# The gMLP row mix's quarter loads: a second place for a21, asked for a pair ahead; a11 asked for ahead of a22

## The chip, the cores and the metric

One core of one Trainium2 chip. The metric is device time in microseconds (us) of one execution of the whole program; lower is better.

## The reference

One sequence of 2048 rows of width 512, all in float32. An attention block, then a gated MLP whose gate mixes rows:

```python
h  = x + attention(layernorm(x)) @ wo            # 32 heads of 16
z  = gelu(layernorm(h) @ w_in)                   # 1376 columns: z1 (688), then z2 (688)
g  = w_sp @ layernorm(z2) + b_sp[:, None]        # w_sp is 2048 x 2048
h2 = h + (z1 * g) @ w_out
```

The change concerns the product `w_sp @ layernorm(z2)`.

## The kernel before

The program runs through four stages: the projections, attention, `make_z` (the MLP's input product, the gelu and the layernorm, up to 1595 us of the span), and the row mix with the output product (from there to the end). Float32 matmuls are made of three: each operand is split into a rounded part and a rest (`parts`: ScalarE writes the rounded part, VectorE the rest), and `mm3` (L87, L88, L89) multiplies high by high, high by low and low by high.

The row mix multiplies by halves with seven products in place of eight. `w_sp` is cut into quarters a11, a12, a21, a22 of 1024 x 1024, and layernorm(z2) into b11, b12, b21, b22 of 1024 x 344. For each **pair** p of row blocks (block p of the upper half and block p of the lower, 128 rows each, p = 0 to 7) the left operands are

- s3 = a11 - a21 (`difference`, L761),
- s1 = a21 + a22, written over a21, and s2 = s1 - a11, written over a11 (`sums`, L761); s2 is also stored to `s_scr` (L783),
- a22 itself, and later a11, a12 and s4 = a12 - s2.

The loop over p from L895 (`for p in range(HB)`) makes four of the products, in TensorE's order g7 = s3 x t3, g6 = s2 x t2, g4 = a22 x n4, g5 = s1 x t1, each of 24 matmuls (8 blocks, three each) of 344 columns. `T` holds t1, t2, t3 and n4, the right operands, made of b. While TensorE makes the products of pair p, the other engines prepare the operands of pair p + 1: `put` splits an operand into one of six places (the slots w0 to w2 and f0 to f2, in rotation). ScalarE's order in one turn of the loop is: the splits of s3, s2, one block of b11 and a22, then `p6` (L952, the copy of g6 out of PSUM), then the split of s1. VectorE's order is: s3, its rest, the sums, the rests of s2, b11 and a22, then `p67` (L953), the rest of s1, and last the three sums `q` (L903, in `keep`) that empty g4 and g5. These orders, and those of TensorE and of the queue SP that issues the loads, are the order of the code (`manual_schedule`): an instruction that waits holds back all behind it on its engine.

PSUM has four buffers for g. The first product of the next pair takes the buffer of g6, which `p6` frees; the second takes that of g7, freed by `p67`; the third and fourth those of g4 and g5, freed by `q`.

A quarter's rows come as two loads of 128 x 512 float32 (256 KB each). `ask(i, j, p, tag)` takes places from a pool by its tag and issues both loads (L747). Tag "rc" has two tiles, so one place, which holds a21; it is free again when both parts of s1 have been made. Tag "o" has one place for a22, free when a22 has been split. Tag "xr" has three tiles for a11, which needs two: the next a11's first half goes into the third tile, its second half into the tile of the present first half, free when s2 has been split and stored. In each turn p, SP issues in this order: the two stores of s2 (L783), the two loads of a22 of pair p + 2, the two of a11, the two of a21, one of b (L874), and the three stores of g (L904).

The last turn (p = 7) has other work: it puts a11 of pair 0 into slot f0 (asked for in turn 6 at the tag "rc"), then splits the sixteen blocks b22 and b21 into the memory of t3 (free after g7) and of t2 (free after g6). Their loads run through six tiles: the sixth b22 block's load waits until the last b11 block has been split, and each of the later ten until a block six earlier has been split. Behind eight of these ten comes a load of 1 MB of w_out (L948), then the last two. The stores of the last g and a reload of pair 0's (`qz`, L980) stand behind those. Then the final loop begins: g1 = a11 x b11, g3 = s4 x b22, g2 = a12 x b21 for each pair, the gate, and the output product; its first transposes (L1035) need `pr`, VectorE's product with z1 (L1073).

Of the kernel before, what the change touches and what calls it, by code (L numbers as in the profile page):

```python
# [8 lines left out]
F32 = mybir.dt.float32  # L9
# [9 lines left out]
P = 128  # L19
# [25 lines left out]
def block_kernel(ctx: ExitStack, tc: tile.TileContext, x, wqkv, wo, w_in, w_sp4, b_sp, w_out, out):  # L45
# [200 lines left out]
    with ExitStack() as pre:  # L246
# [163 lines left out]
        with tc.manual_schedule(engines={E.PE, E.Activation, E.DVE, E.SP}):  # L410
# [47 lines left out]
            for g in range(3):  # L458
                a, b = 4 * g, 4 * g + 4
# [44 lines left out]
            for j in range(24):  # L504
                b, n, i = 1 + j // 8, j // 2 % 4, 1 - j % 2
# [29 lines left out]
    e2 = late.enter_context(tc.tile_pool(name="early_2", bufs=2))  # L535
# [189 lines left out]
    QB = HB // 2  # L725
# [11 lines left out]
    def parts(hi, lo, src, el=None, eh=None):  # L737
        if eh == "pool":
            nc.gpsimd.tensor_copy(hi, src)
        else:  # L740
            nc.scalar.activation(hi, src, AF.Copy)  # L741
        (nc.gpsimd if el == "pool" else nc.vector).tensor_sub(lo, src, hi.bitcast(F32))  # L742

    def load_a(halves, i, j, p):

        for n, t in enumerate(halves):
            nc.sync.dma_start(t, w_sp4[p + HB * i][:, HB * j + QB * n:HB * j + QB * n + QB, :])  # L747

    def cut(t):
        return [t[:, QB * n:QB * n + QB, :] for n in range(2)]  # L750

    def put(slot, halves):

        op = slot.take()
        for n in range(2):
            parts(cut(op[0])[n], cut(op[1])[n], halves[n])
        return op

    def combine(e, out, a, b, op):
        for n in range(2):  # L760
            e.tensor_tensor(out[n], a[n], b[n], op)  # L761

    def half(name, tag, bufs=2):
        return [e2.tile([P, QB, P], F32, name=name, tag=tag, bufs=bufs) for _ in range(2)]

    def ask(i, j, p, tag):

        t = half(f"a{i}{j}", tag, 3 if tag == "xr" else 2)
        load_a(t, i, j, p)
        return t  # L770

    def difference(a11, a21):

        s3 = [e2.tile([P, QB, P], F32, name="s3", tag=f"o2{n}", bufs=1) for n in range(2)]
        combine(nc.vector, s3, a11, a21, ALU.subtract)
        return s3

    def sums(p, a11, a21, a22):

        combine(nc.vector, a21, a21, a22, ALU.add)  # L780
        combine(nc.vector, a11, a21, a11, ALU.subtract)
        for n in range(2):
            nc.sync.dma_start(cut(s_scr[p])[n], a11[n])  # L783

    with ExitStack() as mid:
# [57 lines left out]
        for k in range(NB):  # L843
# [8 lines left out]
            if k == NB - 2:  # L852
                a11, a21, a22 = ask(0, 0, 0, "xr"), ask(1, 0, 0, "rc"), ask(1, 1, 0, "o")
# [6 lines left out]
    with ExitStack() as fin:  # L860
        bc = fin.enter_context(tc.tile_pool(name="fin_b", bufs=1, side="right"))
        fs = fin.enter_context(tc.tile_pool(name="fin_s", bufs=1, side="right"))
        f1 = late.enter_context(tc.tile_pool(name="fin_1", bufs=2))
# [5 lines left out]
        def load_b(i, j, k):  # L869

            staged[0] += 1
            t = (f1.tile([P, FC], F32, name="b", bufs=3) if staged[0] % 2 else
                 e2.tile([P, FC], F32, name="b", tag="hn", bufs=3))
            nc.sync.dma_start(t, z_scr[1][(HB * i + k) * P:(HB * i + k + 1) * P, j * FC:(j + 1) * FC])  # L874
            return t
# [3 lines left out]
        def put_b(b, k, t):  # L879
            parts(b[0][:, k, :], b[1][:, k, :], t)  # L880

        def product(acc, a, b, blocks=range(HB)):
            for k in blocks:
                mm3(acc, a[0][:, k, :], a[1][:, k, :], b[0][:, k, :], b[1][:, k, :],
                    k == 0, k == HB - 1)
# [3 lines left out]
        f = [Slot(fs, f"f{i}") for i in range(3)]  # L889
        ops["s1"] = put(f[0], a21)  # L890
        old, now = [None, None, f[1], f[2]], w + f[:1]
        order = fin.enter_context(tc.manual_schedule(engines={E.PE, E.Activation, E.DVE, E.SP}))
        a11, a21, a22 = ask(0, 0, 1, "xr"), ask(1, 0, 1, "rc"), ask(1, 1, 1, "o")
        b = load_b(0, 0, 0)
        for p in range(HB):  # L895
            nxt, new, last = {}, [old[2], old[3], now[0], now[1]], p + 1 == HB
            ahead = p + 2 if p + 2 < HB else None
            g7, g6, g4, g5 = [ps_g.tile([P, 512], F32, name="g")[:, :FC] for _ in range(4)]
            p6, p67 = [f1.tile([P, FC], F32, name=n) for n in ("p6", "p67")]
            q = [f1.tile([P, FC], F32, name=f"q{i}") for i in range(3)]  # L900

            def keep(i, g, other):
                nc.vector.tensor_add(q[i], g, other)  # L903
                nc.sync.dma_start(g_scr[p][i], q[i])  # L904

            if not last:
                nxt["s3"] = put(new[0], difference(a11, a21))
                sums(p + 1, a11, a21, a22)
                nxt["s2"] = put(new[1], a11)
            else:  # L910
                a11 = put(f[0], a11)
            put_b(b11, p, b)
            if p:
                product(g7, ops["s3"], T["t3"])
            else:
                for blocks in (range(HB - 1), range(HB - 1, HB)):
                    product(g7, ops["s3"], T["t3"], blocks)
                    product(g6, ops["s2"], T["t2"], blocks)
            if not last:
                nxt["a22"] = put(new[2], a22)  # L920

                a22 = ask(1, 1, ahead, "o") if ahead else ask(0, 1, 0, "o")
                if ahead:
                    s2, a11 = a11, ask(0, 0, ahead, "xr")
                else:
                    s2 = half("s4", "xr", 3)
                    for n in range(2):
                        nc.sync.dma_start(s2[n], cut(s_scr[0])[n])
            else:

                b22 = [zc.tile([P, HB, FC], F32R, name="b22", tag=f"t3_{i}") for i in range(2)]
                b21 = []
                asked = [(1, 1, k) for k in range(6, HB)] + [(1, 0, k) for k in range(HB)]

                def put_next(b, k):
                    put_b(b, k, bs.pop(0))
                    if asked:
                        bs.append(load_b(*asked.pop(0)))

                for k in range(6):  # L940
                    put_next(b22, k)
                combine(nc.vector, s2, a22, s2, ALU.subtract)
                s4 = put(f[1], s2)
                for k in range(6, HB):
                    put_next(b22, k)

                raw_u = wc.tile([P, 4, D], F32, name="wr", tag="w2")
                nc.sync.dma_start(raw_u, w_out[:4 * P, :].rearrange("(a p) c -> p a c", p=P))  # L948
                raw_u = [raw_u[:, :2, :], raw_u[:, 2:, :]]
            if p:  # L950
                product(g6, ops["s2"], T["t2"])
            nc.scalar.activation(p6, g6, AF.Copy)  # L952
            nc.vector.tensor_add(p67, g7, p6)  # L953
            if not last:
                nxt["s1"] = put(new[3], a21)
                if ahead:
                    a21 = ask(1, 0, ahead, "rc")
                else:
                    a11 = ask(0, 0, 0, "rc")
                b = load_b(0, 0, p + 1)  # L960
                if not ahead:
                    bs = [load_b(1, 1, k) for k in range(6)]
            else:
                a12 = put(f[2], a22)
                b21 = [zc.tile([P, HB, FC], F32R, name="b21", tag=f"t2_{i}") for i in range(2)]
                for k in range(HB):
                    put_next(b21, k)
                for f0, n in FB[4:]:
                    t = e2.tile([P, D], F32, name="wr", tag="rc")
                    nc.sync.dma_start(t[:n], w_out[f0:f0 + n, :])  # L970
                    raw_u.append(t[:n])
            product(g4, ops["a22"], T["n4"])
            keep(1, g4, p67)
            product(g5, ops["s1"], T["t1"])
            keep(2, g5, p67)
            if last:
                t = zc.tile([P, HB * FC], F32, name="qz", tag="t1_1")
                first = (t[:, :3 * FC].rearrange("p (i c) -> p i c", c=FC),
                         [t[:, (3 + 2 * i) * FC:(5 + 2 * i) * FC] for i in range(2)])
                nc.sync.dma_start(first[0], g_scr[0].rearrange("i p c -> p i c"))  # L980
            keep(0, g5, p6)
            ops, old, now = nxt, now, new
# [6 lines left out]
        t = zc.tile([P, HB * FC], F32R, name="wu5", tag="t1_0")  # L989
# [66 lines left out]
        for p in range(HB):  # L1056
# [17 lines left out]
            if p and not last:  # L1074
                a11 = put(f[0], nxt[1][0])
# [23 lines left out]
            if not p:  # L1099
                a11 = put(f[0], nxt[1][0])  # L1100
# [44 lines left out]
```

## Time and profile before

| | |
|---|---|
| time, median of 3 runs | 1912.09 us (1911.88 to 1912.12) |
| the profiled execution: its own time, its span | 1915.18 us, 1913.1 us |
| TensorE busy, VectorE, ScalarE, GpSimd over the span | 98%, 80%, 69%, 11% |
| mean granted TensorE clock | 0.996 |

Per stretch of the row mix, from the table of windows (us busy, granted clock, mean busy share of the DMA engines):

| stretch, us from the span's start | length | TensorE | VectorE | ScalarE | clock | DMA |
|---|---|---|---|---|---|---|
| 1595 to 1723, the loop over pairs | 128 | 122.47 | 88.12 | 46.96 | 1.00 | 0.57 |
| 1723 to 1742, until the first transposes of the final loop | 19 | 10.67 | 13.13 | 8.22 | 0.82 | 0.72 |
| 1742 to 1913, the final loop | 171 | 166.73 | 92.44 | 45.92 | 0.99 | 0.50 |

How to read the answers: "PE" is TensorE, "DVE" VectorE, "ACT" ScalarE, "SPq" the queue SP. `a <- b: 29.6, 8, 4.6` in the view of waits means that a waited for b for 29.6 us in total, 8 times, the longest 4.6. In the chain of waits and the timeline, the first column is the start in us from the span's start, the second the duration; `[1.65 <-ACT p L952]` is idle time of the engine before the instruction, and who ended it. A DMA in the chain is shown from its issue to its landing.

### The profile page before, as it was taken

What the parts mean: (1) busy time and instruction counts of PE and PEld (TensorE: products, weight loads), DVE (VectorE), ACT (ScalarE), POOL (GpSimd) and SP (SyncE); (2) the same over time, 40 slices, a digit from 0 to 9 for tenths busy, and PEclk for the clock granted to TensorE, in tenths of its full rate; (3) what the DMA queues carried; (4) which work ended last, traced back from release to release, by engine and by line L of the source; (5) the groups of instructions that cost most, each with busy time, mean ns of one, the idle gap of its engine ahead of it and who ended that gap; (6) DMA issues with size and microseconds to landing.
All of it is one profiled execution on the core that took longest, in us unless ns stands there. A gap on an engine that the chain in (4) does not pass through costs nothing.

```text
span 1913.1 us, 32433 instructions
## 1 busy us (share of the span) xinstructions
PE 1881.7 (98%) x11608; PEld 1066.5 (56%) x11608; DVE 1536.7 (80%) x3105; ACT 1328.8 (69%) x1733; POOL 203.1 (11%) x281
## 2 busy tenths in 40 slices
PE   9999999999999999999999999999999999998999
PEld 6865444444444444444444444444349989996887
DVE  6487999999999999999999999999536677766554
ACT  3335888888888888888888888888963344334221
POOL 2130000001011000000000000000014551001211
PEclk9999999999999999999999999999999999998999
DMA  5677111211221111111021021000045554567552
GB/s 186 183 195 188 40 24 31 68 29 28 49 50 33 38 32 23 37 39 24 19 49 35 13 47 33 22 13 5 7 106 154 153 171 153 185 198 245 176 186 77
DMA packets 148105, 159.82 MB, mean 84 GB/s; under 512 B 62952, under 2 KB 92664, under 8 KB 146408
## 3 DMA queue, kind: packets, MB, share of 16 engines
q1 hardware_dynamic: 143304, 146.48, 28.6%
q10 hardware_dynamic: 4608, 11.27, 1.5%
q8 instruction: 91, 1.49, 0.3%
q14 instruction: 70, 0.57, 0.1%
q0 software_dynamic: 32, 0.01, 0.0%
HBM read 101.16 MB, written 55.61 MB: 82 GB/s over the span
## 4 chain that ended last, share of the span: by engine, by line
PE 83%; DMA 6%; DVE 6%; ACT 2%; issue 1%; SPq 1%; ACTq 0%; POOL 0%; DVEq 0%; POOLq 0%
PE pv L619 26%; PE m L203 25%; PE s L608 12%; PE acc L87 5%; PE acc L89 4%; PE acc L88 4%; DMA a<-in_w_sp 2%; DMA h_scr<-xr 2%; PE g L87 2%; PE g L89 1%; PE g L88 1%; DVE ws L742 1%; ACT ws L741 1%; DMA o<-o_scr 1%; PE tp L1035 1%
## 5 line engine op out<-in xcount | busy, mean ns | idle before, releaser
L611 ACT ACTIVATE pt<-s 128x1024 f32<-128x1024 f32 x1024 | 993.1, 1030 | 144.4 <-PE s L608 141.2
L208 DVE TENSOR_REDUCE mx<-m 128x1 f32<-128x512 f32 x1511 | 958.2, 683 | 105.5 <-PE m L203 63.6
L203 PE MATMUL m<-kst,qst 48*128 48x512 f32 x1511 | 607.1, 448 | 0.0
L619 PE MATMUL pv<-pt,vst 128*32 128x512 f32 x4096 | 551.2, 605 | 0.4 <-ACT o L626 0.4
L608 PE MATMUL s<-qst,kst 50*128 50x512 f32 x2048 | 465.9, 428 | 3.1 <-ACT pt L611 2.6
L203 PEld LDWEIGHTS m<-kst,qst 48*128 48x128 f32 x1511 | 263.2, 184 | 315.1 <-DVE mx L208 222.1
L608 PEld LDWEIGHTS s<-qst,kst 50*128 50x128 f32 x2048 | 223.1, 185 | 57.7 <-ACT pt L611 33.2
L203 PE MATMUL m<-uvs,qst 48*128 48x512 f32 x503 | 248.8, 495 | 0.0
L203 PEld LDWEIGHTS m<-uvs,qst 48*128 48x128 f32 x503 | 91.9, 183 | 207.1 <-DVE mx L208 205.2
L217 DVE CUSTOM_DVE_ANT_0 ab<-m,ab 128x512 f32<-128x512 f32 x252 | 171.3, 680 | 3.8 <-ACT ab L213 2.0
L619 PEld LDWEIGHTS pv<-pt,vst 128*32 128x32 f32 x4096 | 83.1, 108 | 161.1 <-issue 154.4
L213 ACT ACTIVATE ab<-m 128x512 f32<-128x512 f32 x251 | 151.1, 602 | 16.7 <-PE m L203 11.1
L81 POOL CAST mparts<-nm 128x16 fp32r<-128x16 f32 x32 | 6.3, 197 | 909.4 <-DVE nm L223 909.4
L741 ACT ACTIVATE ws<-a 128x512 fp32r<-128x512 f32 x80 | 46.4, 624 | 60.1 <-issue 32.1
L87 PE MATMUL acc<-wi,hT 128*128 128x344 f32 x256 | 82.9, 324 | 0.0
L88 PE MATMUL acc<-wi,hT 128*128 128x344 f32 x256 | 81.8, 320 | 0.0
L89 PE MATMUL acc<-wi,hT 128*128 128x344 f32 x256 | 81.8, 319 | 0.0
L87 PE MATMUL g<-b,ws 128*128 128x344 f32 x192 | 65.2, 340 | 4.6 <-DVE q L903 2.9
L742 DVE TENSOR_TENSOR ws<-a,ws 128x512 fp32r<-128x512 f32 x80 | 56.5, 743 | 16.1 <-ACT ws L741 15.9
L87 PE MATMUL g<-t,ws 128*128 128x344 f32 x192 | 62.0, 323 | 4.2 <-ACT p L952 3.6
L741 ACT ACTIVATE ws<-s 128x512 fp32r<-128x512 f32 x32 | 19.3, 630 | 63.7 <-DVE s L761 63.6
L79 ACT ACTIVATE pT<-tp 128x384 fp32r<-128x384 f32 (+2 forms) x48 | 18.3, 382 | 62.7 <-PE tp L1035 45.5
(188 smaller groups left out, 2211.3 us busy)
## 6 DMA issues: line engine op xcount, KB each, us to landing
a<-in_w_sp SPq DMA_DIRECT2D x80, 256.0 KB
qst<-q_scr SPq DMA_DIRECT2D x192, 64.0 KB
kst<-k_scr SPq DMA_DIRECT2D x48, 256.0 KB
z_scr<-z ACTq DMA_DIRECT2D x32, 344.0 KB
k_scr<-part SPq DMA_DIRECT2D x16, 512.0 KB
q_scr<-part SPq DMA_DIRECT2D x16, 512.0 KB
z<-z_scr SPq DMA_DIRECT2D x14, 344.0 KB
b<-z_scr SPq DMA_DIRECT2D x24, 172.0 KB
```

What stands on the lines that cost most here:

```text
L87: nc.tensor.matmul(ps, lh, rh, start=first, stop=False)
L88: nc.tensor.matmul(ps, lh, rl, start=False, stop=False)
L89: nc.tensor.matmul(ps, ll, rh, start=False, stop=last)
L203: nc.tensor.matmul(acc, q[r, p, c], keys[r, p], start=True, stop=True)
L208: nc.vector.reduce_max(at(t, e if t else e - 1), acc, axis=AX.X)
L213: nc.scalar.activation(ab[0], acc, AF.Abs)
L217: nc.vector.tensor_tensor_reduce(ab[0], acc, ab[0], 0.5, LOW, ALU.add, ALU.max, at(0, 0))
L608: nc.tensor.matmul(s[:, t, :], k[r, p, kb * P:(kb + 1) * P], q[r, p, :], start=True, stop=True)
L611: nc.scalar.activation(t, s, AF.Exp, scale=DH ** -0.5)
L619: nc.tensor.matmul(pv[0][32 * j:32 * j + 32, :], vst[hg % 2][:, c:c + 32], pts[j % 2][:, j // 2, :], start=kb == 0, stop=kb == NB - 1)
L741: nc.scalar.activation(hi, src, AF.Copy)
L742: (nc.gpsimd if el == "pool" else nc.vector).tensor_sub(lo, src, hi.bitcast(F32))
```

## The change

a21 gets a second place, the tag "a21" in the pool `f1`. Requests for it alternate between the two places, and each is made at the head of a turn, for the pair after the one whose operands are now prepared; the code that took it at the end of the turn takes the tile asked for. In turn 6 the same early request is for a11 of pair 0, at the tag "rc". The order of the a11 and a22 requests in a turn is exchanged, and so is that of s2's reload, which stands in a11's place in turn 6, and a12's load. Before the loop, pair 1's a21 is asked for first, in the new place.

SP's order in a turn is then: two loads of a21, two stores of s2, two loads of a11, two of a22, one of b, three stores of g. The number of instructions on each engine is the same. TensorE's and ScalarE's orders are the same; on VectorE one thing moves: before the loop's first turn, pair 1's difference now stands ahead of the rests of pair 0's s1.

```diff
-    def half(name, tag, bufs=2):
-        return [e2.tile([P, QB, P], F32, name=name, tag=tag, bufs=bufs) for _ in range(2)]
-
-    def ask(i, j, p, tag):
-
-        t = half(f"a{i}{j}", tag, 3 if tag == "xr" else 2)
+    def half(name, tag, bufs=2, pool=None):
+        return [(pool or e2).tile([P, QB, P], F32, name=name, tag=tag, bufs=bufs) for _ in range(2)]
+
+    def ask(i, j, p, tag, pool=None):
+
+        t = half(f"a{i}{j}", tag, 3 if tag == "xr" else 2, pool)
         load_a(t, i, j, p)
         return t
...
-        a11, a21, a22 = ask(0, 0, 1, "xr"), ask(1, 0, 1, "rc"), ask(1, 1, 1, "o")
+        a21, a11, a22 = ask(1, 0, 1, "a21", f1), ask(0, 0, 1, "xr"), ask(1, 1, 1, "o")
...
             if not last:
+
+                if not ahead:
+                    a = ask(0, 0, 0, "rc")
+                else:
+                    a = ask(1, 0, ahead, "a21", f1) if p % 2 else ask(1, 0, ahead, "rc")
                 nxt["s3"] = put(new[0], difference(a11, a21))
...
                 nxt["a22"] = put(new[2], a22)
 
-                a22 = ask(1, 1, ahead, "o") if ahead else ask(0, 1, 0, "o")
                 if ahead:
-                    s2, a11 = a11, ask(0, 0, ahead, "xr")
+                    a11 = ask(0, 0, ahead, "xr")
                 else:
                     s2 = half("s4", "xr", 3)
                     for n in range(2):
                         nc.sync.dma_start(s2[n], cut(s_scr[0])[n])
+                a22 = ask(1, 1, ahead, "o") if ahead else ask(0, 1, 0, "o")
...
                 nxt["s1"] = put(new[3], a21)
                 if ahead:
-                    a21 = ask(1, 0, ahead, "rc")
+                    a21 = a
                 else:
-                    a11 = ask(0, 0, 0, "rc")
+                    a11 = a
```

## The prediction

> **What bounds the kernel now.** The page first: TensorE is busy nearly all the time, so what can be won is its idle time and its slow clock, and these must be found by stage.
>
> ```profile
> PE 1881.7 (98%) x11608; PEld 1066.5 (56%) x11608; DVE 1536.7 (80%) x3105; ACT 1328.8 (69%) x1733; POOL 203.1 (11%) x281
> ```
>
> The change touches only the row mix, so next TensorE's timeline there. Its rows with idle time are these (two of those at turn ends, of 0.48 and 0.70, and two of 0.29 and 0.44 left out):
>
> ```profile
> 1612.81 0.43 PE L87 MATMUL g<-t,ws 128*128 128x344 f32 x1 [1.65 <-ACT p L952]
> ...
> 1723.31 0.42 PE L87 MATMUL g<-b,ws 128*128 128x344 f32 x1 [1.68 <-ACT p L952]
> 1733.98 0.39 PE L87 MATMUL g<-b,ws 128*128 128x344 f32 x1 [2.90 <-DVE q L903]
> 1742.04 1.51 PE L1035 MATMUL tp<-ident,pr 128*128 128x128 f32 x6 [5.16 <-DVE pr L1073]
> ```
>
> All the waits at turn ends are for `p6`, which stands on ScalarE behind the next pair's splits. Who holds those? The view of waits, from 1590 to 1742 us:
>
> ```profile
> DVE s L761 <- DMA a<-in_w_sp: 29.6, 8, 4.6
> ...
> PEld g L87 <- ACT p L952: 7.2, 7, 2.0
> ACT ws L741 <- DMA a<-in_w_sp: 7.1, 1, 7.1
> ...
> PE g L87 <- DVE q L903: 2.9, 1, 2.9
> ```
>
> The difference s3 waits for rows of a in every turn, and once ScalarE waits 7.1 us for rows to split (a11 of pair 0, turn 7). The chain of waits shows the circle, one turn and then the last:
>
> ```profile
> 1676.97 5.86 DMA a<-in_w_sp
> 1682.92 0.70 DVE s L761
> 1683.73 0.64 ACT ws L741
> 1684.40 1.29 DVE ws L742 x2
> 1685.69 0.67 DVE a L761 x2
> ...
> 1692.60 5.98 DMA a<-in_w_sp
> ...
> 1708.35 5.93 DMA a<-in_w_sp
> 1714.39 1.27 ACT ws L741 x2
> 1716.83 2.39 DMA b<-z_scr
> ...
> 1726.30 6.05 DMA b<-z_scr
> 1733.33 1.34 DVE q L903 x3
> ```
>
> In each turn a21's rows can be asked for only when its one place has been emptied by the last split of the turn, and the next turn's first work waits for them: 15.63 us from request to request (1676.97 to 1692.60), 5.9 of it the load. TensorE needs less: where it doesn't stop (1659.93 to 1689.97, 191 steps) matmuls start 0.1573 us apart, so 96 of them take 15.10. Hence the small waits in every turn. Last, the clock:
>
> ```profile
> 1724.00:1735.00 11.00, 8.10 (x53) 7.85 (x52) 6.61 (x15) 5.87 (x12) 0.00 (x0) 1.00 0.63 204
> 1735.00:1745.00 10.00, 4.84 (x19) 4.37 (x19) 6.45 (x10) 2.14 (x5) 0.91 (x1) 0.50 0.87 282
> ```
>
> The number behind the five engines' busy times is the granted clock: it falls to 0.50 around the long stalls, and matmuls after 1743.2 start 0.29 us apart until 1745.2.
>
> **The first turn.** Before, SP issues two loads of pair 1 at 1582 and then stands until 1601.04, because a21's place is still read by the last rest of pair 0's s1. The new place needs no such wait, but it lies where make_z's data lay, so its load waits for TensorE's last make_z matmul (starts 1594.95, ends 1595.3), and now a11's and a22's loads are queued behind it on SP. Six loads at half a microsecond each: a11's second half, the fourth, goes out at 1597 and lands 4.2 to 6.0 us later (the chain's shortest and longest row), 1601.2 to 1603. Before, the difference's second half began at 1605.84; so pair 1's operands come 3 to 4.5 us earlier, less 1.3 us for the two rests of s1 that VectorE now makes behind the difference. `p6` moves from 1612.3 to 1609 to 1610.6, ahead of 1611.0, where TensorE ends pair 0. The 1.65 us of idle go. The cover is thin at the late end, 0.4 us, but nothing is lost against before.
>
> **The turns 1 to 6.** a21's load is asked for a whole turn earlier than it is used and leaves the circle; I cost it at nothing, and its cover is 15 us against a landing of 6. Two loads move ahead of two stores of s2 on SP. They wait for the split of s1 of the turn before, which is done before the `q` sums, and SP has just waited for those to store them; so SP is not held. What is late next? VectorE now starts a turn when `q` of the last pair is done, about 1.1 us after TensorE goes on to the next pair (the end of g5's last matmul, and two sums of 0.5). From the difference's start to the end of `p6` the trace has 7.7 us (1636.14 to 1643.85). So `p6` ends 8.8 us into a pair of 15.1: 6.3 us of cover. The nearest circle is a11's second half, which waits for the store of s2 out of the tile that it takes: the store goes out 4.7 us after the difference's start (1636.14 to 1640.85), its completion comes 2.0 us after that, and a load of at most 6.0 follows: 12.8 us, against 15.1. a22's rows, now behind a11's, are asked for when a22 has been split, 8.4 us after the difference's start, and are needed 2.8 us after the next start: 14.5 against 17.9. Nothing of these reaches TensorE. The eight pairs then run without a stop: g1 begins at 1595.87 + 8 x 15.10 = 1716.7 instead of 1723.31. **Term 1: 6.6 us.** (The idle times of the timeline add up to 5.24; each also hides 0.16 us, as a matmul's modelled end lies so far behind the next one's usual start: 6.2, the rest are gaps too small to be listed.)
>
> **The last turn.** Here TensorE isn't what is late. Before, ScalarE splits a11 of pair 0 only when its rows land (1714.39), and b11 and b22 after it. Now the rows are asked for at the head of turn 6 and are there by about 1695. The split of b22's first block must then wait for g7 of pair 7 (its memory is t3): TensorE begins pair 7 at 1701.6, and 24 matmuls later, at 1705.5, it is free. Before, that block followed b11's (from 1715.71) at 1716.1; so 10.5 us earlier. The sixth b22 block's load hangs on b11's last split, which moves from 1716.8 to 1704.8 (after the `q` sums at 1703), so its rows are there, and ScalarE's 0.76 us of idle at 1719.24 goes too: 11.2. From there the steps are the old ones: eight loads each freed by a split, the 1 MB of w_out, and the last two b21 blocks behind it, whose rows (the 6.05 us row) release b21's last splits, then `q`, then the reload and `pr`. Moved by 11.2, g4's `q` is done at 1722.7. TensorE ends g1 and g3 at 1716.7 + 48 x 0.157 = 1724.3, so the 2.90 us of idle go; it makes half of g2 by 1726.2 and waits for `pr`, which with its whole chain comes at 1742.04 - 11.2 = 1730.8. **Term 2: 11.2 in all at the first transposes, 4.6 of it beyond term 1.** A lower bound, where the last turn's loads come no faster than before once w_out is under way, is term 1 alone; an upper is 12.
>
> **After that** TensorE has no gap above 0.7 us to 1913 and the loads of the final loop hang on the same chain, so the shift stays. The clock: idle before the transposes shrinks from 5.16 to about 4.4 us. I take the half clock to come again as before, at no difference; if it doesn't, 3.2 us at half speed (1742.04 to 1745.2) save 1.6.
>
> Sum: 11.2, rounded to 11.1 for small new waits. The profiled execution took 1915.18 (span 1913.1 and 2.1 around), the median is 3.1 lower; I take the same saving off the median: 1912.1 - 11.1 = 1901.0.
>
> **Rivals.** (1) *Only the loop gains.* If the b loads and the 1 MB behind them, at a DMA share of 0.87 in 1735 to 1745, set the last turn's end whenever they start, term 2 fails: 1912.1 - 6.6 = 1905.5. Against it: the loads of this turn are issued on splits, not in a block, and DMA share in the loop is 0.57. (2) *The clock stays up*: with a shorter stall 1.6 more, 1899.4. For it: the stall of 1.68 us left the clock at 1.00. Against it: the clock fell at 1735.0 with a single stall of 2.90 behind it. The Trainium skill (TensorE: Matmul & The Clock Gate, Part 1: The HAM clock gate) gives a window of about 3.4 us that runs freely, and half rate after an idle one; by that, 4.4 us of idle may or may not hold a whole window, and the saving would be 11.1 or 12.7. Here the trace is harsher, the clock fell after 2.90 us. (3) *Slower: a11 becomes the circle.* Its second half waits for a store to land, 6.8 us into VectorE's turn, and with a21's loads ahead of it and a22's beside it the load's landing could stretch. A turn is 6.8 us plus that landing: at 8.3 it meets TensorE's 15.1, at 8.8 the turn before, and at 10.4 seven turns cost 14.7, the gain and 3.8 us more: 1916. The longest a row here is 5.98, and the batch it shares is smaller than before (four loads and b in place of six). (4) *The place is not really second*: an address shared with something read late would make SP wait at the head of each turn. The order of instructions shows SP waiting there only for ScalarE's or VectorE's split of the same tag's last user, so no change, 1912, is unlikely.
>
> **Chances.** Forecast 0.72, rival 1 0.10, rival 2 0.08, rival 3 0.05, rival 4 0.05. About 0.2% (3.8 us) is what a measurement can tell: faster 0.90 (forecast and rivals 1 and 2), same 0.05, slower 0.05. The range runs from 1898.5 (12 us and the clock) to 1906.0 (rival 1).
>
> **What would show it.** Right: no wait of the difference for `a<-in_w_sp` in turns 1 to 6, and a wait for TensorE at `q` instead; g<-t matmuls without gaps from 1596 to 1717; ScalarE's 7.1 us wait gone, its first b22 split waiting for TensorE; the first transposes near 1731. Wrong: idle at turn ends that `p6` or a DMA ends, b21's last rows landing later than 1722, or the transposes' shift lost in the final loop.

## The result, and the profile after

| | before | after |
|---|---|---|
| time, median | 1911.99 us (4 runs, 1910.7 to 1912.12) | 1901.36 us (4 runs, 1899.16 to 1902.38) |
| ratio | | 0.9944, 95% interval 0.9927 to 0.9962 |
| profiled execution: time, span, mean clock | 1915.18, 1913.1, 0.996 | 1899.16, 1897.4, 0.998 |

The change saves 10.6 us, by the interval 7 to 14. The forecast was 1901.0.

The two profiled executions differ by more, 15.76 us of span, and 3.95 of that lie ahead of everything that the change touches: the first g matmul begins at 1595.87 before and at 1591.92 after. (In eleven more profiled kernels it begins anywhere from 1589.25 to 1595.16.) So all that follows is counted from the first g of the profile itself:

| us from the first g | before | after | difference |
|---|---|---|---|
| to the first matmul of g1, eight pairs | 127.44 | 121.48 | 5.96 |
| from there to the first transposes | 18.73 | 12.95 | 5.78 |
| from there to the end | 171.10 | 171.03 | 0.07 |
| sum | 317.27 | 305.46 | 11.81 |

TensorE's timeline from 1591 to 1730 us, all of its rows with idle time. Of the eight that before had after the first g, two are left:

```profile
1591.92 0.40 PE L87 MATMUL g<-t,ws 128*128 128x344 f32 x1 [0.59 <-issue]
...
1608.03 0.43 PE L87 MATMUL g<-t,ws 128*128 128x344 f32 x1 [0.81 <-ACT p L957]
...
1726.36 1.51 PE L1040 MATMUL tp<-ident,pr 128*128 128x128 f32 x6 [3.38 <-DVE pr L1078]
```

From 1608.03 to 1722.65 TensorE doesn't stop. The stall of 2.90 before g2 is gone, that before the transposes went from 5.16 to 3.38, and one turn end, the first, still waits for `p6`: 0.81 in place of 1.65.

The view of waits, 1610 to 1700 us:

```profile
ACT ws L741 <- DVE s L761: 33.8, 5, 7.2
DVE q L903 <- PE g L89: 20.5, 11, 3.2
ACT ws L741 <- DVE a L761: 16.3, 6, 2.7
ACT ws L741 <- issue: 5.6, 1, 5.6
```

No wait of the difference for rows of a is left. VectorE now arrives early and waits for TensorE at `q`. ScalarE's wait of 5.6, told as "issue" here, is ahead of the split of a11 of pair 0 into the slot f0; it ends when TensorE has finished pair 6 (the same wait is put down to TensorE in e4 below). In the chain of waits there is no DMA between 1608 and 1703 any more, nearly all of it is TensorE. Its first turn and its last:

```profile
1592.87 6.95 DMA z_scr<-z
1599.96 0.64 ACT ws L741
1600.63 2.50 DVE ws L742 x4
1603.13 1.81 DVE a L761 x3
...
1607.63 0.35 ACT p L957
1608.03 0.43 PE g L87
...
1702.34 0.50 ACT b L741
...
1711.43 4.88 DMA b<-z_scr
1716.34 0.97 ACT b L741 x2
...
1717.76 1.34 DVE q L903 x3
1719.21 0.38 SPq L985
1719.69 4.10 DMA g_scr<-q
...
1726.36 1.51 PE tp L1040 x6
```

The top is new: ScalarE's split of pair 0's s1 waits for a store of make_z. The bottom is the old last turn, earlier. The clock, in the table of windows (length, busy PE, PEld, DVE, ACT, POOL, granted clock, DMA share, GB/s):

```profile
1713.00:1726.00 13.00, 9.97 (x64) 9.68 (x62) 8.33 (x15) 4.36 (x7) 0.00 (x0) 1.00 0.72 245
1726.00:1730.00 4.00, 3.64 (x16) 3.63 (x17) 1.66 (x4) 1.08 (x4) 0.91 (x1) 0.58 0.95 282
```

The half clock still comes behind the transposes: matmuls start 0.29 us apart until 1729.4.

### The profile page after: what moved, and what is told of

It reads as the page before. It is cut to its first block, busy times and chain, and to the rows that moved or that the text cites. A ratio compares the mean times of both kernels' runs of the same rounds, so it can differ in the third digit from the quotient of the medians.

```text
span 1897.4 us, 32426 instructions
## 1 busy us (share of the span) xinstructions
PE 1878.2 (99%) x11608; PEld 1065.5 (56%) x11608; DVE 1537.0 (81%) x3105; ACT 1328.5 (70%) x1733; POOL 203.6 (11%) x281
## 4 chain that ended last, share of the span: by engine, by line
PE 89%; DMA 4%; DVE 3%; ACT 1%; SPq 1%; issue 1%; POOL 0%; ACTq 0%; POOLq 0%; DVEq 0%
PE pv L619 26%; PE m L203 25%; PE s L608 13%; PE acc L87 5%; PE acc L89 5%; PE acc L88 5%; PE g L87 3%; PE g L88 3%; PE g L89 3%; DMA h_scr<-xr 2%; DVE o L84 1%; PE tp L1040 1%; DMA b<-z_scr 0%; ACT pt L611 0%; DVE rs_t L104 0%
## 5 line engine op out<-in xcount | busy, mean ns | idle before, releaser
L87 PE MATMUL g<-b,ws 128*128 128x344 f32 x192 | 64.6, 336 | 0.0
L88 PE MATMUL g<-b,ws 128*128 128x344 f32 x192 | 61.6, 321 | 0.0
```

Of the source, the lines that this page charges most:

```text
L87: nc.tensor.matmul(ps, lh, rh, start=first, stop=False)
L88: nc.tensor.matmul(ps, lh, rl, start=False, stop=False)
```

## The experiments

All are taken from the kernel after or before by the edits shown. The ratio is to the kernel before, timed beside each. The other columns are of the profiled execution, counted as above.

| kernel | ratio, 95% interval | median, us | to g1 | to the transposes | to the end | sum |
|---|---|---|---|---|---|---|
| before | 1 | | 127.44 | 18.73 | 171.10 | 317.27 |
| after | 0.9944 (0.9927 to 0.9962) | 1901.36 | 121.48 | 12.95 | 171.03 | 305.46 |
| e1_place_only | 0.9946 (0.9933 to 0.9959) | 1902.44 | 120.99 | 14.04 | 170.96 | 305.99 |
| e4_loop_only | 0.9934 (0.9920 to 0.9947) | 1900.34 | 121.06 | 13.90 | 172.19 | 307.15 |
| e8_bare_place | 0.9951 (0.9937 to 0.9965) | 1903.20 | 120.99 | 14.96 | 171.98 | 307.94 |
| e2_exchange_only | 0.9960 (0.9947 to 0.9974) | 1906.59 | 121.87 | 16.49 | 171.27 | 309.63 |
| e3_last_turn_only | 0.9981 (0.9972 to 0.9990) | 1910.01 | 126.08 | 18.47 | 171.02 | 315.58 |
| e5_first_turn | 0.9943 (0.9929 to 0.9957) | 1901.79 | 121.14 | 13.70 | 171.15 | 305.99 |
| e11_stores_first | 0.9934 (0.9921 to 0.9946) | 1901.16 | 120.76 | 13.65 | 171.96 | 306.38 |
| e6_w_out_last | 0.9932 (0.9919 to 0.9945) | 1899.61 | 121.00 | 13.64 | 171.20 | 305.84 |
| e9_early_reload | 0.9927 (0.9913 to 0.9941) | 1898.24 | 121.10 | 12.53 | 169.66 | 303.29 |
| e10_both | 0.9931 (0.9917 to 0.9946) | 1898.79 | 121.17 | 11.80 | 169.67 | 302.64 |
| e12_stores_and_reload | 0.9919 (0.9906 to 0.9931) | 1898.23 | 121.26 | 12.64 | 171.20 | 305.09 |

Intervals are some 2.5 us to either side, so what lies closer is told apart, if at all, by the profile, and there a stretch that nothing in a kernel concerns still moves: from the end of the loop to the transposes by a microsecond, with the landing of the last b rows (4.88 us after their request in the change's profile, 5.67 to 6.27 in e1, e4, e5 and e8, all with w_out's 1 MB ahead of them).

### Which part carries it

**The exchange left out** (e1):

```diff
+                a22 = ask(1, 1, ahead, "o") if ahead else ask(0, 1, 0, "o")
                 if ahead:
                     a11 = ask(0, 0, ahead, "xr")
...
-                a22 = ask(1, 1, ahead, "o") if ahead else ask(0, 1, 0, "o")
```

> The change without its exchange: a21's second place and the requests at the head of a turn stay, but a22's rows are asked for ahead of a11's again (and a12's ahead of s2's reload). Theory A (the prediction: the second place takes a21's load out of the circle, the exchange only tidies): as the whole change, 1900 to 1903 us; no wait of the difference for a<-in_w_sp in turns 1 to 6, matmul g1 begins 121 to 122 us after the first g of pair 0. Theory B (the exchange is what counts, because it takes a11's loads out from behind a22's place): most of the gain gone, 1906 us or more, the difference waits for a11's rows 2 to 4 us a turn. Theory C (each of the two parts alone is enough): as the whole change.

Measured: as the whole change, ratio 0.9946 beside 0.9944, and the loop without a stop from the second pair on. From 1610 to 1700 us the difference waits for a's rows three times, 2.2 us in all (and once, 2.4 us, for what is put down to a load of b), and TensorE doesn't notice. Theory B falls.

**The early request left out** (e4):

```diff
-                if not ahead:
-                    a = ask(0, 0, 0, "rc")
-                else:
+                if ahead:
                     a = ask(1, 0, ahead, "a21", f1) if p % 2 else ask(1, 0, ahead, "rc")
...
-                    a11 = a
+                    a11 = ask(0, 0, 0, "rc")
```

> The change without its early request for a11 of pair 0: those two loads go out at the end of turn 6, as before; second place and exchange stay. If the early request carries the last turn's gain (term 2, 4.6 beyond the loop's): ScalarE waits 4 us or more for those rows again, the transposes come 18 to 19 us after g1 begins, 1905 to 1907 us. Rival (once a11's and a21's loads no longer crowd that batch, the rows land in about 4 us, before the split of b22 could start anyway, which waits for g7): no more than 1 us lost, 1901 to 1903 us, and the transposes 13 to 14 us after g1 begins.

Measured: nothing is lost, 0.9934, and the transposes come 13.90 after g1 begins. The view of waits, 1690 to 1700 us, shows why:

```profile
ACT ws L741 <- PE g L89: 5.6, 1, 5.6
```

Although asked for last, the rows of a11 are there before the slot is: the releaser is TensorE's matmul, not a DMA. The rival is right, the request is not what brings the last turn's gain. (The half clock lasted longer in this execution, until 1731, which is the 172.19 at its end.)

**The place alone** (e8) is both edits together.

> The second place alone: a21 alternates between two places and is asked for at the head of a turn; neither the exchange nor the early request for a11 of pair 0. If the place carries the whole gain (what e1 and e4 say one by one): ratio to before 0.994 to 0.995, 1901 to 1904 us, from the first g to the end 305.5 to 307.5 us in the profile, g1 121 to 122 us after the first g, transposes 13 to 15 us after g1 begins. Rival (each of the two others alone is dispensable, but not both, since a11 of pair 0 would then be asked for last, behind a22's place): the last turn loses 3 us or more, ScalarE waits for a<-in_w_sp there, 1905 us or more.

Measured: 1903.20 us, in the theory's range, though the ratio, 0.9951, and the profile's 307.94 lie just outside theirs (0.995 and 307.5). The sum of the profile is 2.5 us above the whole change; 0.9 of that is a longer half clock, and the last b rows landed after 6.27 us in place of 4.88. With neither part, ScalarE does wait for a11's rows, as the rival has it, and yet little comes of it. ScalarE's timeline:

```profile
1699.24 1.25 ACT L741 ACTIVATE ws<-a 128x512 fp32r<-128x512 f32 x2 [7.10 <-DMA a<-in_w_sp]
1700.40 0.49 ACT L741 ACTIVATE b<-b 128x344 fp32r<-128x344 f32 x1
1701.44 2.01 ACT L741 ACTIVATE b<-b 128x344 fp32r<-128x344 f32 x5 [0.56 <-PE g L89]
```

The wait is as long as in the kernel before, but the whole turn is earlier: the first b22 split behind it must still wait 0.56 for TensorE's g7, and comes 109.9 us after the first g (110.4 in the whole change). The length of a wait doesn't tell its price. A small one may be left: the last b rows are asked for 13.7 us after the start of pair 7 here, 12.7 in e1 and in e4, 13.1 in the whole change. Whether the two parts bring 1 to 2 us or none is not settled; the intervals overlap for most of their length.

**The exchange alone** (e2): the kernel before with the two requests exchanged, as in the last but one piece of the change's diff; a21 is still asked for at the end of the turn, in its one place.

> The kernel before with the exchange alone: a11's rows are asked for ahead of a22's, a21 keeps its one place and is asked for last in the turn. Theory A: the circle through a21's place stays (9.7 us from the load's landing to the next request, then a load of 5.9), so the loop keeps its 15.6 us a pair: 1911 to 1913 us, the difference waits for a<-in_w_sp in every turn for 2 to 4 us. Theories B and C: before, a21's request shared its batch with a11's four loads, which stood behind the wait for a22's place; with a11 gone ahead, only a22 and b go out beside it, its load lands in about 4 us, the circle is 9.7 + 4 = 13.7, below TensorE's 15.1, and the loop runs without stops from turn 1 on. Only the first turn keeps its idle 1.7: 1900 + 1.7, thus 1902 to 1905 us if the last turn goes with it, 1906 to 1908 if not (a11 of pair 0 is asked for at the end of turn 6 here).

Measured: 0.9960, some 7 us faster, two thirds of the change, and no stop in the loop behind the first turn. Theory A falls here: one place is enough for that. But the difference still waits, as theory A says (waits, 1612 to 1695 us):

```profile
DVE s L761 <- DMA a<-in_w_sp: 19.4, 7, 3.7
```

So the circle is still there; it has only become shorter than TensorE's turn. From the end of one `p6` to the next it takes 14.4 us (31.24 to 88.86 us behind the first g, four turns), against 15.6 before and TensorE's 15.04. The 9.7 us from the start of the difference to the next request are unchanged (1643.22 to 1652.88); the load shrank: its rows release the difference 4.3 to 5.3 us after the request (1652.88 to 1657.22, 1637.92 to 1643.22), where the rows of before in the chain are 5.1 to 6.0. Before, four loads of a11 and a22 went out in the 2 us ahead of it (1643.95 to 1645.93), since a11's stood behind the wait for a22's place; now they go out over 4 us (1648.97 to 1652.88), and the first have landed, or nearly, when a21's starts. The expectation had 4 and 13.7. In the last turn a circle of 14.4 is not enough: a11 of pair 0 is asked for only 1.4 us before pair 7 begins (1696.39 and 1697.74), where e4, which has the second place and no early request either, asks 5.3 us ahead. ScalarE waits 5.0 and then 1.0 us for those rows, work arrives 2 to 3 us later than with two places, `p6` of the last turn ends at 119.8 in place of 117.2, and the transposes come 16.49 after g1 begins. That is what a second place buys beside the exchange. For the loop theory C is left: either part alone takes the stops out.

**The early request alone** (e3): in the kernel before, a11 of pair 0 is asked for at the head of turn 6, in a place of its own.

> The kernel before with one thing: a11 of pair 0 is asked for at the head of turn 6, in a place of its own (the change's new one). a21 keeps its one place, a22's rows stand ahead of a11's. All theories: the loop keeps its waits (the difference for a<-in_w_sp, TensorE's stops of 0.3 to 1.7 us at turn ends, g1 begins 127 us after the first g). Prediction's term 2: ScalarE's wait of 7.1 us in the last turn goes, its first b22 split waits for g7, and the transposes come 4 to 5 us earlier relative to the start of g1: 1907 to 1908 us. Rival (the b loads and the 1 MB behind them set the end of the last turn whenever they start): 1911 to 1912 us.

Measured: the loop keeps its stops, and the stretch behind it its length, 18.47 (18.73 before), where term 2 had promised 4 to 5 us less. ScalarE's timeline in the last turn:

```profile
1711.01 1.49 ACT L741 ACTIVATE b<-b 128x344 fp32r<-128x344 f32 x3 [4.99 <-DMA b<-z_scr]
```

a11's rows are there and split, and ScalarE waits for b's instead, whose request stands at the end of the turn, as late as before (1705.97, landed 1710.99). The time is lower all the same, by 2 to 5 us, and the profile shows 1.7 of that, 1.36 within the loop, where nothing was meant to change. Where it comes from stays open.

### The stall that stayed in the first turn

**Another order before the loop** (e5):

```diff
-        a21, a11, a22 = ask(1, 0, 1, "a21", f1), ask(0, 0, 1, "xr"), ask(1, 1, 1, "o")
+        a11, a21 = ask(0, 0, 1, "xr"), ask(1, 0, 1, "a21", f1)
         b = load_b(0, 0, 0)
+        a22 = ask(1, 1, 1, "o")
```

> The whole change with another order before the loop: pair 1's a11 first, then a21 in the new place, then the b rows, which wait until 1595, and a22 last. Theory (the idle 0.5 to 1.0 us left in the first turn is the landing of the last z_scr store, 6.5 to 7.0 us, because six loads go out beside it; with two it lands after about 4.5): ScalarE splits s1 about 2 us earlier, p6 is ahead of the end of pair 0 and the step at pair 0's end falls from 1.1 (0.7 in two other runs) to 0.3 or less: 0.5 to 1.0 us faster than the whole change, 1900 to 1901 us. Rival (the store is slow for another reason, or a22's rows, now asked for 2 us later, hold the sums): the step stays at 0.7 to 1.1 or grows, 1901 to 1903 us.

Measured: no effect. b's rows didn't wait, a22's followed half a microsecond later, and the store found as much beside it as before: it landed after 6.58. The step at the end of pair 0 (from its last matmul's start to that of pair 1's first) is 0.78, 0.46 of it idle; e1, e4 and e8, whose first turn is that of the change, have 0.66 to 0.70, the change 1.12. The edit didn't make the condition that it was to test, so it says nothing on the theory.

**The stores on SP** (e11):

```diff
-            nc.scalar.dma_start(z_scr[0][rows, :], z[0])
+            (nc.sync if sb == 2 * HB - 1 else nc.scalar).dma_start(z_scr[0][rows, :], z[0])
...
-            nc.scalar.dma_start(z_scr[1][rows, :], z[1])
+            (nc.sync if sb == 2 * HB - 1 else nc.scalar).dma_start(z_scr[1][rows, :], z[1])
```

> The whole change, with make_z's last two z_scr stores issued by SP behind a21's first load and ahead of the other five, in place of ScalarE's queue; on VectorE pair 1's difference then stands behind the rests of pair 0's s1, as in the kernel before. Theory (the last z_scr store lands after 6.5 to 7.0 us in place of 2.25 because its transfer stands behind the loads issued just before it): it lands within 2.3 to 4.5 us, ScalarE's split of s1 begins 2 us earlier or more, and the step at the end of pair 0 falls from 0.7 to 1.1 to 0.2 or less: 0.5 to 0.9 us faster than the whole change, ratio 0.993 to 0.994, which only the profile can tell apart. Rival (a11's second half, now the last but behind the stores, becomes late): the store lands early, but the difference waits for a<-in_w_sp until 1 to 2 us later than now, and the step stays at 0.7 or grows.

Measured: the store lands after 3.63 us, with one load ahead of it in place of four. So its 6.5 to 7.0 come from its place among the loads. But the chain now goes through the loads that it passed, as the rival has it:

```profile
1597.66 5.88 DMA a<-in_w_sp
1603.57 0.70 DVE s L761
1604.29 0.64 ACT ws L741
...
1610.55 0.42 PE g L87
```

The step at the end of pair 0 is 0.41, between the two forecasts, and 0.93 with the same edit in e12. What the store gains, a11's second half loses: the two halves of a21, the two of a11 and the store are all needed there, whatever their order.

### What sets the end of the last turn

**w_out's 1 MB behind the last b21 rows** (e6): the load at L953 is moved behind the loop over b21.

> The whole change, with the 1 MB load of w_out moved behind the last two b21 loads. Theory (the prediction's first rival in part: the 1 MB ahead of them makes the last b21 rows late, and these set the end of the last turn): the last b21 rows land 2.4 to 3 us after their request in place of 4.9 to 6.1, b21's last splits, q, the reload and the transposes come 2 to 2.5 us earlier, 1899 to 1900 us. Rival (the rows of w_out then land later, and their splits stand ahead of pr on ScalarE and VectorE): the b21 splits come earlier, but the transposes no more than 1 us, 1900 to 1902 us.

Measured: the last b rows land 2.4 us after their request (1708.44 to 1710.84), `q` follows at 1711.82, and the transposes come no earlier, 13.64 after g1 begins. The view of waits, 1705 to 1725 us:

```profile
ACT wu L741 <- DMA wr<-in_w_out: 5.3, 1, 5.3
DVE wu L742 <- ACT wu L741: 4.6, 1, 4.6
```

The wait moved to w_out's own rows, whose splits stand ahead of `pr`. The time, 1899.61, lies in the theory's range, but with 2.5 us of interval it can't tell the two apart; by the profile the rival is right.

**The reload before the stores** (e9): in the last turn, qz's three loads are issued as soon as g5 has been made, in front of the stores that wait for `q`.

```diff
             product(g5, ops["s1"], T["t1"])
-            keep(2, g5, p67)
             if last:
                 t = zc.tile([P, HB * FC], F32, name="qz", tag="t1_1")
...
                 nc.sync.dma_start(first[0], g_scr[0].rearrange("i p c -> p i c"))
+                for i in (1, 0):
+                    nc.sync.dma_start(first[1][i], z_scr[0][HB * i * P:(HB * i + 1) * P, :])
+                keep(1, g4, p67)
+            keep(2, g5, p67)
             keep(0, g5, p6)
```

(`keep(1, ...)` stays in its old place in the other turns, and the two loads of z_scr that stood behind the loop are gone.)

> The whole change, and in the last turn the reload of pair 0's g and z rows (qz) is issued before the three stores of the last g instead of between and behind them, as its memory is free when TensorE has made g5. Theory (the step of 3.7 us before the first transposes is the reload behind the stores that wait for q): it goes out 5 us earlier and lands before VectorE has split w_out; VectorE then makes pr right behind those splits, 1.3 us earlier, so 1900 us, and 1898.5 if the shorter stall also keeps the clock up. Rival (the reload now lies beside the last b21 rows and w_out and delays them by as much): no gain, 1901 to 1903 us, the last b21 rows landing later than 4.9 to 6.1 us after their request.

Measured: the best of those with one edit, 1898.24, 0.9927, though its interval reaches to the change's. It gains in two places. `pr` begins 0.4 us behind VectorE's splits of w_out in place of 1.35, and the clock doesn't fall: from the transposes to the end it takes 169.66, 1.4 less than before and after. TensorE's timeline:

```profile
1726.82 0.85 PE L1042 MATMUL tp<-ident,pr 128*128 128x128 f32 x6 [2.97 <-DVE pr L1080]
```

and the table of windows, with the granted clock third from the right:

```profile
1724.00:1730.00 6.00, 3.19 (x21) 3.12 (x22) 3.74 (x8) 1.74 (x5) 0.92 (x1) 1.00 0.68 216
```

**e10 and e12** are e9 with e5's and with e11's edit.

> The first-turn order and the early reload together, on top of the whole change: if each brings what its theory says, 1898.5 to 1900 us and 2 us below the whole change; if neither, 1901 to 1903 us.

> The early reload of qz (1898.2 us as a run by itself, ratio 0.9927) and the z_scr stores on SP together. If both add up: step at the end of pair 0 0.2 or less, and the clock at full speed behind the transposes: ratio 0.992 to 0.9925, 1897 to 1898 us. If the stores bring nothing: as the early reload alone.

Measured: 1898.79 and 1898.23 us, e9 over again; the first-turn edits bring nothing on top. In e12 the idle time before the transposes is 3.07, and there the clock did fall:

```profile
1725.64 1.32 PE L1042 MATMUL tp<-ident,pr 128*128 128x128 f32 x6 [3.07 <-DVE pr L1080]
```

Why there and not in e9? By the granted clock that the traces record, each stretch at half clock in these kernels, but for the last, which the end of the trace cuts off, lasts 3.41 us (after, e12), 6.83 (e4, e8) or 10.24 (before): once, twice or three times the same length. Cut into pieces of 3.41 us, with their borders where the recorded changes of the clock have them, e12's stall lies in one piece and e9's on a border. The table of windows for the two pieces of e12, then those of e9:

```profile
1722.45:1725.86 3.41, 0.34 (x3) 0.25 (x3) 3.30 (x7) 0.55 (x1) 0.00 (x0) 1.00 0.43 96
1725.86:1729.28 3.42, 3.42 (x15) 3.37 (x14) 1.09 (x3) 1.16 (x4) 0.91 (x1) 0.50 0.91 312
...
1721.71:1725.12 3.41, 2.13 (x14) 1.85 (x12) 3.02 (x5) 0.00 (x0) 0.00 (x0) 1.00 0.37 128
1725.12:1728.54 3.42, 1.73 (x13) 1.75 (x14) 2.34 (x5) 1.04 (x2) 0.92 (x1) 1.00 0.84 259
```

TensorE, the first number behind the length, was busy for 0.34 us of the piece at whose end the clock fell, and for 2.13 and 1.73 us of the two that share e9's stall. So of e9's two gains the reload's 1 us is the edit's, while the 1.4 us of the clock are in part luck: they hang on where the stall lies as well as on its length. In e10, with 2.23 us of stall, no piece had less than 1.89 us of work.

## Why the prediction was right, point by point

**The sum** was 11.1; the medians give 10.6, the profile 11.8 from the first g on. That the forecast is only 0.4 us off is partly luck: in the profile term 1 came out 0.6 us smaller than forecast and term 2 1.2 us larger, some 1 us of that because the last b rows landed sooner in this one execution.

**The first turn** failed in the sentence "The 1.65 us of idle go." 0.81 stayed in the change's profile, 0.3 to 0.6 in the other kernels with two places but for e11, which lists none. a11's second half landed after 6.64 us where the step had 4.2 to 6.0, at 1599.38 or 7.5 us behind the first g (5.3 to 7.1 forecast), but that was the smaller miss: the step named only the difference as late. ScalarE's order puts the split of pair 0's s1 ahead of that of s3, into slot f0, whose memory the last store of make_z still reads. That store landed after 2.25 us before and 6.95 now, beside the six loads that had been moved there. It was not in the sum, and it cost 0.96 (a step of 1.12 at the end of pair 0 in place of 0.16).

**The turns 1 to 6** were right in size: the prediction had `p6` end 8.8 us into a pair, and it ends after 8.66 (54.97 behind the first g, in a pair that begins at 46.31). a11's second half, the circle of rival 3, landed after 3.2 to 4.2 us where 8.3 would have been needed.

**Term 1** was 6.6 and came to 5.96: the 0.96 of the first turn was lost, and pairs of 15.04 us in place of 15.10 gave some of it back.

**Term 2** was 4.6 beyond term 1 and came to 5.78; 4.7 to 5.0 in e1, e4 and e5. Its last b rows landed after 4.88 us where the row of before had 6.05. Its size was right, its cause was not: the step says "Now the rows are asked for at the head of turn 6" and hangs all else on it. e3 has that request and gains nothing behind the loop; e4 lacks it and loses nothing. What brings the last turn forward is the loop's work ahead of TensorE: once the difference no longer waits for a21, turn 6 with its requests runs ahead of TensorE. Even asked for in its old place, in e4, a11 of pair 0 is requested 5.3 us before pair 7 begins (1691.11 and 1696.40), where before it was 2.0 us behind (1708.35 and 1706.33). Then the first b22 split waits for g7 as forecast, 110.4 us behind the first g (the prediction had 1705.5 - 1595.87 = 109.6).

**The circle** was rightly seen, and one way out of it overlooked. The prediction took the landing of 5.9 as given and left the load's place in its batch at no worth. e2 shows that the exchange by itself takes 1.2 us off the circle, enough to bring it under TensorE's turn. The two parts don't add up: with two places the exchange is worth nothing that can be measured (e1).

**The clock** came back to half behind the transposes, at no difference (171.03 and 171.10), as forecast. Rival 2 was wrong for the change, but its price was about right: where the clock stays up, in e9 and e10, 1.4 us are saved (1.6 forecast). The Trainium skill (TensorE: Matmul & The Clock Gate, Part 1: The HAM clock gate) has a window of about 3.4 us that runs freely of the program, with half rate after an idle one. The traces agree with the first half of that: half clock comes in pieces of 3.41 us, and stalls of nearly one length end differently by where they lie (2.97 without a fall in e9, 3.07 with one in e12). They don't agree with a wholly idle window as the condition: before, the clock fell at 1735.02 behind 3.41 us of which TensorE had been busy for 1.04. How much work keeps the clock up no run settles.

**Rival 1** was wrong, as term 2 came, and rival 4, as the loop runs without its circle: the new place is a second one.

## What to carry to other kernels

A load that waits for its place closes a circle of work, request and landing; compare its length with the turn of the engine that sets the time, and cut whichever piece is cheapest. Moving other requests out of its way in the queue may be enough; a second place takes the load out of the circle altogether. A long wait in the profile has a price only if what stands behind it is not held by something else anyway: the same 7.1 us that stood in the chain of the last turn before cost about 1 us, by the profile, once the turn was early. And loads that become free to start early land beside somebody else's transfer: look for what waits on that one.

## What the runs showed of the hardware

A store issued by ScalarE among loads issued by SP landed in the order of issue with them, not by itself, in all eight kernels here that have such a batch: in the profile after, by the completions in the trace, eight transfers issued from 1591.36 to 1593.78 landed in just that order, at 1595.2, 1596.9, 1597.4, 1597.9, 1599.4, 1599.8, 1600.1 and 1600.8, ScalarE's two being the third and the sixth. The Trainium skill (DMA: Bandwidth & Descriptors, Issuing engines are not separate DMA queues) says that DMAs of all engines run on the same DMA engines and interleave; the trace agrees, with 6.95 us beside the loads and 2.25 without them for the same 344 KB, and with packets of both moved side by side, 147 of the loads' and 123 of the store's from 1597.5 to 1599.0.
